# The last group's second product in seven parts, with its first product interleaved, in a fused retention and squared-ReLU kernel

## The chip, the cores and the metric

The kernel runs on one core of one Trainium2 chip. The metric is the device time of one execution, in microseconds (us); several executions are taken of each kernel, the kernel before and the changed one on the same chip, and the medians are quoted. The span of a profile is about 2 us shorter than the time of the same execution.

Engine names in the profile: PE is TensorE (matrix products), PEld its weight loads, DVE is VectorE, ACT is ScalarE, POOL is GpSimd, SP is SyncE. A "q" behind an engine's name means its instruction queue, which also issues stores.

## The reference, cut to what matters

```python
attn_out = retention(q, k, v)                  # (8, 8, 576, 64)
x = attn_out.transpose(0, 2, 1, 3).reshape(4608, 512)
h = x @ w_in                                   # (4608, 2048)   "first product"
r = np.maximum(h, 0.0)
g = r * r
out = g @ w_out                                # (4608, 512)    "second product"
```

The 4608 rows are cut into 36 units of 128 rows. Two units make a group, so there are 18 groups. A unit is either 128 rows that lie together ("full") or two blocks of 64 rows from two batches ("tail"). The last group holds a full unit, 34, and a tail unit, 35.

## The kernel before

The kernel writes no fixed order. It registers tasks with an engine, a sort key, a duration and dependences; a small list scheduler in Python then fixes the order of instructions for each engine. The sort key decides which of several ready tasks goes first. From group 2 on, the second product of a group is done in seven smaller products of half by half by half (Strassen's scheme in Winograd's form) instead of eight, with sums of blocks on DVE. The last group is the exception: it has the plain second product.

```python
def add_ff(g):                       # first product, ReLU, square, second product
    base = us[0] * L
    ...
    on_act = n == 2 and g >= STRASSEN and fb in SQ_ACT        # 7 of 8 squares on ACT
    ...
    if STRASSEN <= g < len(groups) - 1:
        add_strassen(g, us, base2, sq)
        return
    for s, u in enumerate(us):       # plain second product: groups 0, 1 and the last
        cuts = [(0, DM)] if u != groups[-1][-1] else [(0, HM), (HM, DM)]
        ...                          # 16 matmuls of 512 columns, or 2 x 16 of 256
        nc.scalar.copy(out=tile_of["o", u][:, lo:hi], in_=tile_of["po", u, lo])
        ...                          # store, issued by ACT in the last group
```

PSUM is the memory into which TensorE writes its products; a bank is one piece of it. In the seven-part scheme three PSUM banks serve all parts. The parts run in the order 1, 7, 6, 2, 5, 3, 4, so that part 6 is the third in time, and parts 3 and 4 are the sixth and the seventh. Bank a takes parts 1, 6, 5 and 3 in turn, and the sum so far is copied out by ACT between them:

```python
p5 = product(5, 16, "a", summed(0), wT[0], ...)
c4 = on_act_copy("u4", "a", 21, [p5])
d22 = on_dve_add(uB, 1, "c", "u4", 22, [p7, c4], ("o",))
p3 = product(3, 20, "a", summed(3), wB[1, 1], ..., [c4])       # waits for the copy
c12 = add("ACT", base + 25, 0.37, f12, deps=[p3, d11])
p4 = product(4, 24, "c", raw(1, 1), wT[3], high, ..., [d22])   # waits for the addition
```

## Time and profile before

| | kernel before |
|---|---|
| time, median of the first 3 runs | 298.69 us (298.68 to 298.79) |
| span of the profiled run | 296.6 us |
| TensorE busy | 286.1 us (96%) |
| last matmul ends | 293.46 us |
| from there to the end of the span | 3.14 us |

The table reads like this: TensorE works to 293.46 us almost without a break, and then 3.14 us pass in which the last result is copied out of PSUM, stored, and the program ends. The views that show it are in the prediction. One more, the sums over a stretch of time, gives the load of the other engines while the last two groups are worked on (columns: stretch, its length, then busy time and number of instructions of PE, PEld, DVE, ACT and POOL, the granted clock, the DMA share and GB/s):

```profile
268.60:286.50 17.90, 17.90 (x165) 16.00 (x164) 5.10 (x12) 14.65 (x28) 0.00 (x0) 1.00 0.16 60
```

ACT is busy for 14.65 of 17.90 us and DVE for 5.10.

### The profile page before, as it was taken

Reading aid. Unit: us, or ns where it says so; the run is one execution under the profiler, and the core shown is the slowest. Engines: PE = TensorE matmul, PEld = TensorE weight load, DVE = VectorE, ACT = ScalarE, POOL = GpSimd, SP = SyncE. Lnnn points to the kernel's source line nnn. Section 1 sums busy time; section 2 is a strip of 40 time slices with the busy share of each in tenths; the row PEclk is TensorE's granted clock in tenths of the full one; section 3 lists DMA queues with packets and bytes.
Section 4 is the critical chain, followed back from the end, with each engine's and each line's share of the span. In section 5 each row is a group of like instructions: output and inputs, shape, how many; then the busy total and the mean of one; then the engine's idle time right before and its main releaser. Section 6 shows DMA issues by size and latency. Waiting matters only on the chain.

```text
span 296.6 us, 10048 instructions
## 1 busy us (share of the span) xinstructions
PE 286.1 (96%) x4320; PEld 233.5 (79%) x4320; DVE 196.2 (66%) x413; ACT 187.5 (63%) x354; POOL 93.9 (32%) x129
## 2 busy tenths in 40 slices
PE   8979999999989999999999999999999999999995
PEld 3558755688878888888788888788888888888874
DVE  4777469967495959593959596766786766462410
ACT  5257753474867676648576667756666666658861
POOL 4454384544232506062414142435141520000000
PEclk9999999999999999999999999999999999999999
DMA  7999998899999989999969698999898980101012
GB/s 205 326 373 385 361 270 220 207 202 180 200 148 216 195 195 169 212 196 199 180 163 160 157 190 206 206 201 205 142 215 140 219 133 32 73 3 71 2 71 73
DMA packets 139261, 54.14 MB, mean 183 GB/s; under 512 B 118096, under 2 KB 130640, under 8 KB 139216
## 3 DMA queue, kind: packets, MB, share of 16 engines
q1 hardware_dynamic: 138768, 52.97, 86.2%
q8 instruction: 34, 0.56, 0.8%
q10 hardware_dynamic: 448, 0.52, 0.6%
q14 instruction: 11, 0.09, 0.1%
HBM read 36.70 MB, written 9.44 MB: 156 GB/s over the span
## 4 chain that ended last, share of the span: by engine, by line
PE 64%; DVE 11%; ACT 10%; DMA 9%; issue 2%; POOL 2%; POOLq 0%
PE po L912 26%; PE ph L819 25%; DVE gS L890 5%; ACT rl L827 5%; ACT gT L837 4%; PE psO L337 4%; PE po L860 4%; DMA pair<-in_v_dram 3%; DMA wo<-in_moe_w_out_dram 3%; DMA pair<-in_k_dram 3%; PE warm L241 2%; DVE gT L839 2%; PE psc L337 1%; PE psS L337 1%; PE psT L412 1%
## 5 line engine op out<-in xcount | busy, mean ns | idle before, releaser
L819 PE MATMUL ph<-xT,w_in 128*128 128x256 f16 x1152 | 139.3, 273 | 0.0
L819 PEld LDWEIGHTS <-w_in 128*128 128x128 f16 x1152 | 111.2, 98 | 14.8 <-POOL w_in L316 0.3
L827 ACT ACTIVATE rl<-ph 128x512 f16<-128x512 f32 x144 | 84.1, 588 | 51.4 <-PE ph L819 48.9
L837 ACT ACTIVATE gT<-rl 128x512 f16<-128x512 f16 x112 | 70.6, 630 | 3.4
L890 DVE TENSOR_TENSOR gS<-gT 128x512 f16<-128x512 f16 x60 | 31.8, 531 | 40.3 <-ACT gT L837 39.7
L912 PEld LDWEIGHTS <-gS 128*128 128x128 f16 x480 | 45.6, 98 | 9.8 <-DVE gS L890 4.5
L912 PE MATMUL po<-wT,gS 128*128 128x256 f16 x360 | 49.2, 273 | 2.0 <-DVE gS L890 1.9
L361 POOL TENSOR_TENSOR v<-v,vdec_full 128x512 f16<-128x512 f32 x24 | 26.2, 1092 | 58.4 <-DMA v<-in_v_dram 51.0
L912 PEld LDWEIGHTS <-gT 128*128 128x128 f16 x360 | 34.7, 98 | 4.2
L912 PE MATMUL po<-w_out,gT 128*128 128x256 f16 x240 | 31.1, 273 | 0.0
L349 POOL CAST kq<-k 128x512 f16<-128x512 f32 x28 | 19.0, 677 | 36.9 <-DMA k<-in_k_dram 35.6
L839 DVE TENSOR_TENSOR gT<-rl 128x512 f16<-128x512 f16 x32 | 18.1, 568 | 13.8 <-ACT rl L827 13.4
L349 POOL CAST kq<-q 128x512 f16<-128x512 f32 x28 | 18.1, 647 | 23.3 <-DMA q<-in_q_dram 23.2
L860 PE MATMUL po<-w_out,gT 128*128 128x512 f16 (+1 forms) x112 | 22.6, 349 | 0.1
L925 ACT COPY u<-po 128x256 f32<-128x256 f32 x30 | 11.0, 367 | 15.5 <-PE po L912 15.4
L935 DVE TENSOR_TENSOR o<-po,u 128x256 f32<-128x256 f32 x30 | 12.6, 419 | 11.8 <-PE po L912 8.1
L698 DVE TENSOR_TENSOR xT<-psO,gam_full 128x512 f16<-128x512 f32 x28 | 18.4, 684 | 2.7 <-PE psO L337 2.5
L637 DVE TENSOR_TENSOR rT<-psc,mask 128x512 f16<-128x512 f32 x28 | 18.5, 681 | 1.4 <-PE psc L337 1.4
L890 DVE TENSOR_TENSOR gS<-gS,gT 128x512 f16<-128x512 f16 x30 | 16.3, 544 | 1.0
L860 PEld LDWEIGHTS <-gT 128*128 128x128 f16 x112 | 10.6, 98 | 7.9 <-issue 0.2
L912 PE MATMUL po<-wT,gT 128*128 128x256 f16 x120 | 15.8, 273 | 0.0
L890 DVE TENSOR_TENSOR gS<-gT,gS 128x512 f16<-128x512 f16 x30 | 15.1, 505 | 1.0
(78 smaller groups left out, 264.2 us busy)
## 6 DMA issues: line engine op xcount, KB each, us to landing
out_dram<-o SPq DMA_DIRECT2D x31, 256.0 KB, 3.1
k<-in_k_dram SPq DMA_DIRECT2D x24, 256.0 KB, 4.9
q<-in_q_dram SPq DMA_DIRECT2D x24, 256.0 KB, 4.9
v<-in_v_dram SPq DMA_DIRECT2D x24, 256.0 KB, 4.6
wi<-in_moe_w_in_dram SPq DMA_DIRECT2D x4, 1024.0 KB, 9.9
wo<-in_moe_w_out_dram SPq DMA_DIRECT2D x4, 1024.0 KB, 9.5
pair<-in_k_dram SPq DMA_DIRECT2D x4, 512.0 KB, 5.7
pair<-in_q_dram SPq DMA_DIRECT2D x4, 512.0 KB, 5.4
```

Source lines behind the costliest of these rows:

```text
L337: nc.tensor.matmul(out_, lhsT=lhsT, rhs=rhs, start=start, stop=True, skip_group_check=True, tile_position=(64 * row, 64 * col))
L349: op(out=out_.rearrange("p (n b a d) -> p n b a d", n=2, b=2, a=2), in_=in_.rearrange("p (n a b) d -> p n b a d", n=2, a=2))
L361: nc.gpsimd.tensor_tensor(out=t, in0=tile_of["v32", u], in1=vdec[kind].rearrange("p (h o) -> p h o", o=1).to_broadcast([P, H, D]), op=ALU. ...
L637: nc.vector.tensor_tensor(out=r, in0=tile_of["psc", g][:, :, cols(s)].rearrange("p a (n i) -> p a n i", i=64), in1=mask.rearrange("p (o r ...
L698: nc.vector.tensor_tensor(out=tile_of["x", g][:, :, s * P:(s + 1) * P].rearrange("p n (c i) -> p c n i", c=2), in0=tile_of["psO", g][:, :, ...
L819: nc.tensor.matmul(tile_of["ph", g, fb][:, j, :], lhsT=w_in16[:, m, fi * P:(fi + 1) * P], rhs=tile_of["x", g][:, m, :], start=(m == 0), st ...
L827: nc.scalar.activation(out=t, in_=tile_of["ph", g, fb], func=ACTF.Relu)
L837: nc.scalar.activation(out=t, in_=rl, func=ACTF.Square)
L839: nc.vector.tensor_tensor(out=t, in0=rl, in1=rl, op=ALU.mult)
L860: nc.tensor.matmul(tile_of["po", u, lo], lhsT=tile_of["g", g][:, fi, s * P:(s + 1) * P], rhs=w_out16[:, fi, lo:hi], start=(fi == 0), stop= ...
L890: nc.vector.tensor_tensor(out=Sx(k, h), in0=in0(h), in1=in1(h), op=op)
L912: nc.tensor.matmul(tile_of["pb", g, bank], lhsT=left(i), rhs=right[:, i, :], start=(start and i == 0), stop=(i == HF - 1), skip_group_chec ...
```

## The change

The intent is to save an eighth of the last group's second product, the only one since group 2 that was still plain. That product stands at the very end, so two things are added to keep TensorE from waiting there. The last group's first product is interleaved with the second product of the group in front, so that its squares are ready sooner; and parts 3 and 4 get banks of their own, so that they need not wait for a copy or an addition. The squares of the last two groups move mostly from ACT to DVE, and the outputs are stored in quarters, as each becomes ready, half from ACT and half from SP.

```diff
+    SPREAD = 0.9
+    SQ_LATE = (1, 4, 6)
...
-        base = us[0] * L
+        base = min(us) * L
+        def place(x):
+            return base + x if g < last_g else base - NF * n - 1 + SPREAD * x
...
-            on_act = n == 2 and g >= STRASSEN and fb in SQ_ACT
+            on_act = g >= STRASSEN and fb in (SQ_ACT if g < last_g - 1 else SQ_LATE)
...
-        if STRASSEN <= g < len(groups) - 1:
+        if STRASSEN <= g:
             add_strassen(g, us, base2, sq)
             return
... (in add_strassen)
+        if g == last_g:
+            d7 = add("DVE", base + 18, 0.42, f7, deps=[p7, c2], acq=("p1",))     # p1 <- bank c + u2
+            d22 = on_dve_add(uB, 1, "c", "u4", 22, [c4, d7])
+            p3 = product(3, 20, "d", summed(3), wB[1, 1], lambda h: [s4[h]], True, True, [])
+            p4 = product(4, 24, "e", raw(1, 1), wT[3], high, True, True, [])
+            c12 = on_dve_add(uA, 1, "d", "u4", 25, [p3, d22])
+            d21 = on_dve_add(uB, 0, "e", "p1", 29, [p4, d22])
+        else:
             ...                                       # as before
+                for d in ds:
+                    lo = 0 if d in (d11, d21) else HM
+                    eng = ("ACT", ...) if d in (c12, d22) else ("SP", ...)
+                    ...                               # one store for each quarter
```

Here uA is the tail unit 35 and uB the full unit 34. Each store of a quarter of the tail unit is two instructions, one for each block of 64 rows.

More of the change, by code (lines that the diff above doesn't have):

```diff
@@ L784, with store @@
     wT_done = t1 + t2 + t3 + t4
-    def store(u, o, lo=0, hi=DM):
+    def store(u, o, lo=0, hi=DM, eng=nc.sync):
         kind, b, c = units[u]
-        eng = nc.scalar if group_of[u] == len(groups) - 1 else nc.sync
         if kind == "full":
@@ L820, in f @@
                                          rhs=tile_of["x", g][:, m, :], start=(m == 0), stop=(m == NP - 1))
-                f1.append(add("PE", base + (nf * fb + j) * n, 0.01 + 0.2133 * n, f,
+                f1.append(add("PE", place((nf * fb + j) * n), 0.01 + 0.2133 * n, f,
                               deps=[T["x", u] for u in us] + wcast_of(nf * fb + j) + f1[-1:],
@@ L839, in fg @@
                     nc.vector.tensor_tensor(out=t, in0=rl, in1=rl, op=ALU.mult)
-            r = add("ACT", base + 4 * fb + 4, 0.6, fr, deps=[f1[-1]], acq=("rl",))
+            r = add("ACT", place(4 * fb + 4), 0.6, fr, deps=[f1[-1]], acq=("rl",))
             sched.free("ff", [r])
-            sq.append(add("ACT" if on_act else "DVE", base + 4 * fb + 6, 0.63 if on_act else 0.45, fg, deps=[r] + sq[:1],
+            sq.append(add("ACT" if on_act else "DVE", place(4 * fb + 6), 0.63 if on_act else 0.45, fg, deps=[r] + sq[:1],
                           acq=() if fb else ("g",)))
@@ L852, in add_ff @@
             f2 = T["ff2"][-1:] if s == 0 else f2[-1:]
-            cuts = [(0, DM)] if u != groups[-1][-1] else [(0, HM), (HM, DM)]
-            for ci, (lo, hi) in enumerate(cuts):
-                for fi in range(NF):
-                    def f(fi=fi, s=s, u=u, lo=lo, hi=hi):
-                        if fi == 0:
-                            tile_of["po", u, lo] = ps_ff.tile([P, hi - lo], FP32, name="po", tag="ff")
-                        nc.tensor.matmul(tile_of["po", u, lo], lhsT=tile_of["g", g][:, fi, s * P:(s + 1) * P],
-                                         rhs=w_out16[:, fi, lo:hi], start=(fi == 0), stop=(fi == NF - 1))
-                    f2.append(add("PE", base2 + NF * s + fi / len(cuts) + 8 * ci, 0.0025 + 0.2135 / len(cuts), f,
-                                  deps=[sq[fi // nf]] + wcast[4 + fi // 4] + f2[-1:],
-                                  acq=("ff",) if fi == 0 else ()))
-                def fo(u=u, lo=lo, hi=hi):
-                    if lo == 0:
-                        tile_of["o", u] = o_pool.tile([P, DM], FP32, name="o", tag="o")
-                    nc.scalar.copy(out=tile_of["o", u][:, lo:hi], in_=tile_of["po", u, lo])
-                oc = add("ACT", end + 1, 0.12 + 0.47 / len(cuts), fo, deps=[f2[-1]], acq=() if lo else ("o",))
-                sched.free("ff", [oc])
-                st = add(*(("ACT", end + 1.1, 0.05) if g == len(groups) - 1 else ("SP", -0.5, 0.7)),
-                         lambda u=u, lo=lo, hi=hi: store(u, tile_of["o", u], lo, hi), deps=[oc], after=2.5)
@@ new lines, in add_ff, with f @@
+            for fi in range(NF):
+                def f(fi=fi, s=s, u=u):
+                    if fi == 0:
+                        tile_of["po", u] = ps_ff.tile([P, DM], FP32, name="po", tag="ff")
+                    nc.tensor.matmul(tile_of["po", u], lhsT=tile_of["g", g][:, fi, s * P:(s + 1) * P],
+                                     rhs=w_out16[:, fi, :], start=(fi == 0), stop=(fi == NF - 1))
+                f2.append(add("PE", base2 + NF * s + fi, 0.216, f, deps=[sq[fi // nf]] + wcast[4 + fi // 4] + f2[-1:],
+                              acq=("ff",) if fi == 0 else ()))
@@ L874, in add_ff, with fo @@
+            def fo(u=u):
+                tile_of["o", u] = o_pool.tile([P, DM], FP32, name="o", tag="o")
+                nc.scalar.copy(out=tile_of["o", u], in_=tile_of["po", u])
+            oc = add("ACT", end + 1, 0.59, fo, deps=[f2[-1]], acq=("o",))
+            sched.free("ff", [oc])
+            st = add("SP", -0.5, 0.7, lambda u=u: store(u, tile_of["o", u]), deps=[oc], after=2.5)
             sched.free("o", [st])
@@ L949, in add_strassen, with f7, f12 @@
         c4 = on_act_copy("u4", "a", 21, [p5])
-        d22 = on_dve_add(uB, 1, "c", "u4", 22, [p7, c4], ("o",))
-        sched.free("u4", [d22])
-        p3 = product(3, 20, "a", summed(3), wB[1, 1], lambda h: [s4[h]], False, True, [c4])
-        def f12():
-            nc.scalar.copy(out=o_tile(uA)[:, HM:], in_=bank("a"))
-        c12 = add("ACT", base + 25, 0.37, f12, deps=[p3, d11])
-        sched.free("ff", [c12])
-        p4 = product(4, 24, "c", raw(1, 1), wT[3], high, False, True, [d22])
-        d21 = on_dve_add(uB, 0, "c", "u2", 29, [p4, d22])
-        sched.free("ff", [d21])
-        sched.free("u2", [d21])
+        if g == last_g:
+            def f7():
+                t = tile_of["p1", g] = u_pool.tile([P, HM], FP32, name="p1", tag="p1")
+                nc.vector.tensor_tensor(out=t, in0=bank("c"), in1=tile_of["u2", g], op=ALU.add)
+            d7 = add("DVE", base + 18, 0.42, f7, deps=[p7, c2], acq=("p1",))
+            sched.free("u2", [d7])
+            d22 = on_dve_add(uB, 1, "c", "u4", 22, [c4, d7])
+            sched.free("ff", [d22])
+            sched.free("ff", [c4])
+            p3 = product(3, 20, "d", summed(3), wB[1, 1], lambda h: [s4[h]], True, True, [])
+            p4 = product(4, 24, "e", raw(1, 1), wT[3], high, True, True, [])
+            c12 = on_dve_add(uA, 1, "d", "u4", 25, [p3, d22])
+            d21 = on_dve_add(uB, 0, "e", "p1", 29, [p4, d22])
+            d22["acq"] = ("o",)
+        else:
+            d22 = on_dve_add(uB, 1, "c", "u4", 22, [p7, c4], ("o",))
+            sched.free("u4", [d22])
+            p3 = product(3, 20, "a", summed(3), wB[1, 1], lambda h: [s4[h]], False, True, [c4])
+            def f12():
+                nc.scalar.copy(out=o_tile(uA)[:, HM:], in_=bank("a"))
+            c12 = add("ACT", base + 25, 0.37, f12, deps=[p3, d11])
+            sched.free("ff", [c12])
+            p4 = product(4, 24, "c", raw(1, 1), wT[3], high, False, True, [d22])
+            d21 = on_dve_add(uB, 0, "c", "u2", 29, [p4, d22])
+            sched.free("ff", [d21])
+            sched.free("u2", [d21])
         sched.free("wst", [p3])
@@ L965, in add_strassen @@
         for u, ds in ((uA, [d11, c12]), (uB, [d22, d21])):
-            st = add("SP", -0.5, 0.7, lambda u=u: store(u, o_tile(u)), deps=ds, after=2.5)
-            sched.free("o", [st])
+            if g < last_g:
+                st = [add("SP", -0.5, 0.7, lambda u=u: store(u, o_tile(u)), deps=ds, after=2.5)]
+            else:
+                st = []
+                for d in ds:
+                    lo = 0 if d in (d11, d21) else HM
+                    eng = ("ACT", base + 25.1, 0.05) if d in (c12, d22) else ("SP", -0.5, 0.05)
+                    st.append(add(*eng, lambda u=u, lo=lo, eng=eng: store(u, o_tile(u), lo, lo + HM,
+                                                                          nc.scalar if eng[0] == "ACT" else nc.sync),
+                                  deps=[d], after=2.5))
+            sched.free("o", st)
     for g in range(len(groups)):
```

## The prediction

> **What bounds the kernel now.** I read the page first: the share of each engine and the slices over the span.
>
> ```profile
> PE 286.1 (96%) x4320; PEld 233.5 (79%) x4320; DVE 196.2 (66%) x413; ACT 187.5 (63%) x354; POOL 93.9 (32%) x129
> ...
> PE   8979999999989999999999999999999999999995
> ```
>
> TensorE is busy for 96% of a span of 296.6 us and falls only in the last slice. A busy TensorE is not proof of a bound, so I went on to the chain of work that ended last, from 255 us to the end. Its columns are the start, the length and the work.
>
> ```profile
> 268.60 4.80 PE ph L819 x44
> 273.40 1.75 PE po L912 x16
> 275.15 1.31 PE ph L819 x12
> 276.46 0.44 PE po L912 x4
> 276.89 0.87 PE ph L819 x8
> ...
> 281.26 1.75 PE po L912 x16
> 283.01 3.49 PE ph L819 x32
> 286.50 6.96 PE po L860 x48
> 293.46 0.02 issue
> 293.48 0.37 ACT o L869
> ```
>
> Each piece begins where the one before it ended, and all of them are TensorE until 293.46 us. There is no wait to be removed here: the end moves only if TensorE is given less to do, or if what follows its last matmul changes. The first product (ph) has a steady pace: 4.80 / 44 = 0.1091 us for one matmul of 256 columns. The last row is the last group's second product: 16 matmuls of 512 columns for one unit, then 2 x 16 of 256 for the other. At 0.1091 us the 32 narrow ones take 3.49 us, so the 16 wide ones take 6.96 - 3.49 = 3.47 us, 0.217 us each: a column costs the same in both widths.
>
> Third, the timeline of the last microseconds (start, length, engine, work):
>
> ```profile
> 286.34 7.11 PE L860 MATMUL po<-w_out,gT 128*128 128x512 f16 x48
> 286.84 0.63 ACT L837 ACTIVATE gT<-rl 128x512 f16<-128x512 f16 x1
> 287.37 0.58 ACT L827 ACTIVATE rl<-ph 128x512 f16<-128x512 f32 x1
> 287.99 0.43 DVE L839 TENSOR_TENSOR gT<-rl 128x512 f16<-128x512 f16 x1 [4.52 <-ACT rl L827]
> ...
> 293.48 0.37 ACT L869 COPY o<-po 128x256 f32<-128x256 f32 x1 [1.19 <-PE po L860]
> 293.88 0.34 ACTq L792 DMA_DIRECT2D out_dram<-o  x1
> ```
>
> From the last matmul's end to the end of the span there are 296.6 - 293.46 = 3.14 us: the copy out of PSUM ends at 293.85, the store is issued at 293.88, and 2.72 us follow. The view of DMA issues, from 293.8 us on, says how much of that is the store itself:
>
> ```profile
> out_dram<-o ACTq DMA_DIRECT2D x1, 128.0 KB, 1.7
> ```
>
> The store lands 1.7 us after its issue, which leaves 1.0 us in which the program ends. The rows also show that the first product of the last group hands over its last square at 288.4 us, 2 us into the second product. The plain second product takes the blocks in order, so this lateness costs nothing today. The new product wants the late blocks sooner.
>
> **What the Trainium skill says.** "TensorE: Matmul & The Clock Gate", section "Back-to-back issue gap", gives N / 2.4 + 2.5 ns as the isolated gap of a warm matmul, which is 109.2 ns for 256 columns and 215.8 ns for 512. The trace agrees: 109.1 and 217 ns. The same section gives about 131 ns as the sustained spacing at 512 columns; this trace does not show that, and I use the trace. "Perfetto Trace Analysis", section "Matmuls", says that independent matmul groups should rotate through different PSUM banks, so that the emptying of one overlaps the matmuls of the next; banks of their own for the last two parts are that rule. "DMA: Bandwidth & Descriptors", section "Issuing engines are not separate DMA queues", says that stores issued from two engines share the same 16 DMA engines and that only sequencer time is saved. No row of the trace before tests that, since its last stores all come from one queue.
>
> **The change part by part.**
>
> *Second product in seven parts.* The old one streams 16 x 512 + 32 x 256 = 16,384 columns. The new one has 7 products of 8 matmuls of 256 columns, 56 x 256 = 14,336 columns. The difference is that of 8 narrow matmuls: 8 x 0.1091 = 0.87 us off TensorE, in the one place where every microsecond is on the path. The new length is 56 x 0.1091 = 6.11 us.
>
> *Additions.* DVE gets 8 sums of 128x512 (0.42 to 0.43 us each in rows of this kind) and 5 additions of 128x256 (0.42 us), and more squares: 10 of the 16 squares of the last two groups go to DVE instead of 2. That is 8 x 0.43 + 5 x 0.42 + 8 x 0.43 = 9.0 us more on DVE. From 268.6 to 286.5 us DVE was busy 5.1 us of 17.9, so there is room. ACT loses 8 squares (5.0 us) and the output copies, and gains three 0.37 us copies. None of it is on the path unless TensorE waits for it.
>
> *Interleaving.* The order of instructions in the built program confirms it: the last group's 64 first-product matmuls are spread in fours and eights among the 56 of the group in front, and only 2 matmuls of that group follow the last of them. Nothing is removed by this. It makes the squares ready earlier relative to the second product, which the sums need.
>
> *Does TensorE wait?* I laid the last rows out by hand, with zero at the end of the last first-product matmul. TensorE then has 2 matmuls of the group in front, 8 of the first part, 8 of the second, and 4 of the third before it needs the last sum: 22 x 0.1091 = 2.40 us. On the other side: ReLU 0.04 to 0.64; DVE first does an output addition that waits for the 2 matmuls (0.25 to 0.67); square to 1.12; the sum with the late blocks to 1.58; the sum built on it to 2.04. That is 0.36 us early. The remaining waits are looser: the bank of the last part was freed by an addition that follows the fourth part, over 1 us earlier, and the parts that share a bank with a copy have a whole other part (0.87 us) between them, against 0.37 us of copying. Earlier in the interleaved stretch the closest wait is a bank that a ReLU must empty, some 0.4 us ahead. So I expect no TensorE wait, and the 0.87 us arrive.
>
> *After the last matmul.* Before: 0.02 + 0.37 (ACT copy) + 0.03 + 2.72 = 3.14 us. After: 0.03 + 0.42 (DVE addition) + 0.03 + 2.72 = 3.20 us, now through the SP queue. Just ahead of it ACT issues the tail unit's right half as two stores. Two such issues took 1.20 us before, so the second begins about 0.2 us after the last matmul and ends about 0.8 us after it; it lands at nearly the same moment as the last store. Three stores of 128 KB then meet in about 1.4 us; at the 330 to 346 GB/s that the last store reached alone, each occupies 0.4 us. I add 0.05 us for that. The loss is 0.11 us.
>
> Sum: -0.87 + 0.06 + 0.05 = -0.76 us, and 298.69 - 0.76 = 297.9 us.
>
> **The rivals.**
>
> First, **a wait takes the place of the removed work**: the sums or a bank come late and TensorE stands before the third part. For it: the slack is only 0.36 us, less than one ACT instruction (0.6 us), and both ACT and DVE run in order with other groups' work between. Against it: ACT had all of its first-product work, with 7 squares in a group, and still kept up to within 2 us; it is now relieved. One ACT instruction in the way would cost 0.6 - 0.36 = 0.24 us, giving 298.2 us; two would cost 0.84 us and leave 298.8 us.
>
> Second, **the tail grows**: the pair on the ACT queue, or the SP queue's own wait, lands after the last addition's store. For it: the rows of stores in two pieces show 0.55 to 0.60 us of issue for each piece against 0.35 us for a whole one. Against it: they start earlier. If the pair's second piece landed 2.3 us after its issue, the shortest that the trace shows for such pieces, it would do so at 0.2 + 2.3 = 2.5 us, against 0.48 + 1.7 = 2.2 us for the last store. That would add 0.3 us: 298.2 us.
>
> Third, **the interleaving itself pays or costs**: TensorE changes bank and weights source every 2 to 8 matmuls. Pieces of 4 in the chain before took 0.44 us, the steady pace, so I give it nothing. Nor can it pay by filling gaps, since the chain has none there. If each of some 25 changes cost 10 ns, the time would be 298.1 us.
>
> **Range and chances.** The main term is a count times a steady pace, so it can hardly be off by more than 0.05 us. The rivals all take back, by 0.2 to 0.8 us; a few tenths can also be gained if the end of the program is shorter after the SP queue. I take 297.5 to 298.4 us. A change of 2% would need 6 us, several times all that is being moved, so within 2% is nearly certain.
>
> **What would show it right or wrong.** Right: the chain shows 56 matmuls in about 6.1 us at the end with no wait on ACT or DVE between them; TensorE's last matmul ends near 292.6 us; DVE's last addition is 0.42 us and some 2.7 us follow its store. Wrong, first rival: a gap before the third part, with DVE sums named as its releaser. Wrong, second: over 3.4 us from the last matmul to the end. Wrong, third: the interleaved stretch runs slower than 0.109 us a matmul. The prediction as a whole fails if the time is not 0.3 to 1.2 us lower.

## The result

The changed kernel took 299.25 us in the median of six runs (298.73 to 299.64), the kernel before 298.69 us (298.44 to 298.79) in six runs on the same chip. The ratio of the changed kernel's time to that of the one before is 1.0019, with a 95% interval of 1.0007 to 1.0032. A ratio is the mean time of one kernel's fast runs over that of the other's of the same rounds, so it is not quite the ratio of the medians. The time lies above the predicted range (297.5 to 298.4 us), and the direction is the opposite of the predicted one.

The profiled run is the fastest of the six (298.73 us). First the page's busy times:

```profile
PE 284.7 (96%) x4328; PEld 234.0 (79%) x4328; DVE 205.3 (69%) x434; ACT 182.9 (62%) x346; POOL 93.2 (31%) x129
```

DVE has 9.1 us more than before (9.0 were predicted) and ACT 4.6 us less (squares of 5.0 us were to leave it). The sums over the same stretch as above, now with DVE at 9.14 us, show that the moved work found room:

```profile
268.62:286.30 17.68, 17.68 (x164) 15.85 (x163) 9.14 (x23) 12.00 (x22) 0.00 (x0) 1.00 0.08 31
```

The chain of work that ended last (start, length, work), in the stretch that the change reorders:

```profile
281.50 0.22 PE po L910 x2
281.72 0.44 PE ph L823 x4
282.15 0.22 PE po L910 x2
...
284.34 1.53 PE po L910 x14
285.87 0.44 PE ph L823 x4
286.30 6.35 PE po L910 x58
292.65 0.02 issue
292.67 0.42 DVE o L933
```

The interleaving stands there, mostly in twos and fours, at the same 0.109 us a matmul, and no other engine comes between. The last 58 matmuls (2 of the group in front and 56 of the seven parts) take 6.35 us. The last matmul ends at 292.65 us. This is the predicted place (292.6), and 0.81 us earlier than before.

So the gain arrived on TensorE and is lost behind it. From the last matmul to the end of the span there are now 296.4 - 292.65 = 3.75 us instead of 3.14. The timeline of these last microseconds:

```profile
291.79 0.38 ACTq L792 DMA_DIRECT2D out_dram<-o  x1
292.26 1.17 ACTq L796 DMA_DIRECT2D out_dram<-o  x2
292.67 0.42 DVE L933 TENSOR_TENSOR o<-po,p 128x256 f32<-128x256 f32 x1 [0.45 <-PE po L910]
293.12 0.34 SPq L792 DMA_DIRECT2D out_dram<-o  x1
```

The last store is issued at 293.12, and 3.28 us follow it (2.72 before). The second line is the tail unit's right half, two stores by ACT, whose issues last until 293.43: the "late pair" from here on. The view of DMA issues from 288 us on (size of one, us from issue to landing):

```profile
out_dram<-o SPq DMA_DIRECT2D x2, 64.0 KB, 2.0
out_dram<-o ACTq DMA_DIRECT2D x1, 128.0 KB, 1.8
out_dram<-o ACTq DMA_DIRECT2D x2, 64.0 KB, 2.1
out_dram<-o SPq DMA_DIRECT2D x1, 128.0 KB, 2.2
```

The last store takes 2.2 us to land; the last store of the kernel before took 1.7.

A gain of 0.8 us and a loss of 0.6 us leave 0.2 us less, but the median is 0.56 us more. The profiled run, the fastest of the six, can't show why. There are thus two questions: what makes the end longer, and where the rest comes from.

### The profile page after: what moved, and what is told of

Its sections match the earlier page's. It is cut to its first block, busy times and chain, and to the rows that moved or that the text cites. A ratio compares the mean times of both kernels' runs of the same rounds, so it can differ in the third digit from the quotient of the medians.

```text
span 296.4 us, 10095 instructions
## 1 busy us (share of the span) xinstructions
PE 284.7 (96%) x4328; PEld 234.0 (79%) x4328; DVE 205.3 (69%) x434; ACT 182.9 (62%) x346; POOL 93.2 (31%) x129
## 4 chain that ended last, share of the span: by engine, by line
PE 62%; DVE 12%; DMA 11%; ACT 8%; issue 3%; POOL 2%; SPq 0%; POOLq 0%; DVEq 0%
PE po L910 27%; PE ph L823 27%; DVE gS L888 5%; ACT rl L831 4%; PE psO L339 4%; ACT gT L841 4%; DMA wo<-in_moe_w_out_dram 3%; DMA pair<-in_v_dram 3%; DMA pair<-in_k_dram 3%; DMA pair<-in_q_dram 2%; PE psc L339 1%; DVE gT L843 1%; PE po L861 1%; PE psS L339 1%; DVE o L933 1%
## 5 line engine op out<-in xcount | busy, mean ns | idle before, releaser
L841 ACT ACTIVATE gT<-rl 128x512 f16<-128x512 f16 x104 | 65.5, 630 | 3.2
L910 PEld LDWEIGHTS <-gS 128*128 128x128 f16 x512 | 48.9, 98 | 9.6 <-DVE gS L888 3.9
L910 PE MATMUL po<-wT,gS 128*128 128x256 f16 x384 | 53.0, 273 | 1.7 <-DVE gS L888 1.3
L910 PEld LDWEIGHTS <-gT 128*128 128x128 f16 x384 | 37.2, 98 | 4.9 <-issue 0.3
L910 PE MATMUL po<-w_out,gT 128*128 128x256 f16 x256 | 33.5, 273 | 0.0
L843 DVE TENSOR_TENSOR gT<-rl 128x512 f16<-128x512 f16 x40 | 21.0, 527 | 15.2 <-ACT rl L831 14.7
L888 DVE TENSOR_TENSOR gS<-gT,gS 128x512 f16<-128x512 f16 x32 | 18.6, 585 | 1.0
L888 DVE TENSOR_TENSOR gS<-gS,gT 128x512 f16<-128x512 f16 x32 | 17.8, 556 | 1.1
L910 PE MATMUL po<-w_out,gS 128*128 128x256 f16 x128 | 16.6, 273 | 0.0
L861 PE MATMUL po<-w_out,gT 128*128 128x512 f16 x64 | 15.5, 379 | 0.2 <-POOL w_out L318 0.2
```

Source lines behind the costliest of these rows:

```text
L841: nc.scalar.activation(out=t, in_=rl, func=ACTF.Square)
L843: nc.vector.tensor_tensor(out=t, in0=rl, in1=rl, op=ALU.mult)
L861: nc.tensor.matmul(tile_of["po", u], lhsT=tile_of["g", g][:, fi, s * P:(s + 1) * P], rhs=w_out16[:, fi, :], start=(fi == 0), stop=(fi == N ...
L888: nc.vector.tensor_tensor(out=Sx(k, h), in0=in0(h), in1=in1(h), op=op)
L910: nc.tensor.matmul(tile_of["pb", g, bank], lhsT=left(i), rhs=right[:, i, :], start=(start and i == 0), stop=(i == HF - 1), skip_group_chec ...
```

## The experiments

Two numbers serve for all of them. The first is the **matmul stretch**, from the start of the last retention output products, which stand ahead of everything the change touches, to the end of the last matmul. The second is the **tail**, from there to the end of the span. The start is read in the timeline as the first row of this kind, here in the kernel before and in the changed one:

```profile
261.82 0.21 PE L337 MATMUL psO<-kqT,Rm 64*64 64x64 f16 x1
```

```profile
261.84 0.21 PE L339 MATMUL psO<-kqT,Rm 64*64 64x64 f16 x1
```

The stretch is 293.46 - 261.82 = 31.64 us before and 292.65 - 261.84 = 30.81 us after. All that both numbers leave out is the same program in both kernels: the order of instructions in the built programs is equal up to that point on every engine.

| run | edit | start, us | stretch, us | tail, us | sum, us |
|---|---|---|---|---|---|
| before | | 261.82 | 31.64 | 3.14 | 34.78 |
| b1_before | none, again | 262.90 | 31.63 | 3.07 | 34.70 |
| b3_inter | interleaving alone | 262.58 | 31.64 | 3.08 | 34.72 |
| after | the change | 261.84 | 30.81 | 3.75 | 34.56 |
| a1_again | none, again | 260.35 | 30.80 | 3.85 | 34.65 |
| c4_after | none, again | 261.07 | 30.80 | 3.73 | 34.53 |
| a2_queues | issuing engines exchanged | 262.96 | 30.81 | 3.73 | 34.54 |
| a3_nopair | late pair left out | 262.16 | 30.81 | 3.13 | 33.94 |
| b4_full | late pair doubled in bytes | 262.08 | 30.80 | 4.02 | 34.82 |
| c2_tiny | late pair, few bytes | 262.14 | 30.80 | 3.56 | 34.36 |
| d2_tinysplit | few bytes, two engines | 261.64 | 30.81 | 3.35 | 34.16 |
| b2_split, c3_split | late pair from two engines | 262.14, 262.41 | 30.80, 30.81 | 3.36, 3.28 | 34.16, 34.09 |
| d1_one | late pair as one store | 262.20 | 30.80 | 5.60 | 36.40 |
| a4_nointer | without the interleaving | 261.70 | 31.17 | 3.83 | 35.00 |
| c1_banks | without banks of their own | 262.44 | 31.42 | 3.74 | 35.16 |

The views print a span to 0.1 us, so a tail or a sum of the table can be off by 0.05 us. Read unrounded from the kept traces, the tail is 3.12 to 3.13 us in the kernel before, b1_before and b3_inter, 3.78 to 3.82 in the changed kernel, a1_again and c4_after, 3.16 in a3_nopair, 3.71 in a2_queues, 3.54 in c2_tiny, 3.32 in d2_tinysplit, and 3.33 and 3.34 in b2_split and c3_split. Equal programs thus repeat the stretch within 0.02 us and the tail within 0.04 us. The start moves by 2.6 us between executions, although nothing in front of it differs.

### a1_again, b1_before and c4_after: both kernels once more

The edit is none: the changed kernel twice more, and the kernel before as a run of its own. The question is whether 0.56 us slower is a property of the change.

> The changed kernel unaltered, for a second trace: the first trace fell in its fastest execution (298.73 us, where the median is 299.25). Theory A (the loss is in the stores after the last matmul, several of which are under way at once): the last matmul ends near 292.7 us again and 4.2 to 4.8 us follow it, against 3.75 in the first trace. Theory C (the loss is somewhere earlier in the program, from the loads or instruction fetch, and varies): the last matmul ends 0.4 to 0.9 us later than 292.65 and about 3.7 us follow. Time 299.0 to 299.4 under both.

> The kernel before, as a run of its own, for a second trace of it and for the spread of its times beside its own copies. From the start of the last output products that both kernels share (261.82 us in the first trace) to the last matmul: 31.64 us again, within 0.05; from the last matmul to the end 3.14 us, within 0.1. If that start itself moves by up to 1 us or more between traces, as it did in the four traces of the changed kernel and its variants (260.35 to 262.96), then the spread of the whole time belongs to the part that the change doesn't touch, and the two kernels can be told apart by the two stretches alone. Ratio to its own copies: 1.000, within the interval.

> The changed kernel unaltered, a third set of times. If the first comparison (0.56 us slower in the median) was due to the spread of the untouched part, the ratio lies within 0.997 and 1.003 with both signs possible, and the stretches are 30.81 and 3.75 to 3.85 us again. If the change really slows the untouched part, the ratio comes out at 1.001 or more a second time and the start of the shared products, as the difference of the span and the two stretches, lies 0.5 us or more above that of the kernel before.

Measured, as medians: a1_again 297.94 us against 298.42, ratio 0.9995 (0.9959 to 1.0031); c4_after 298.33 us against 298.90, ratio 0.9990 (0.9965 to 1.0014); b1_before 299.38 us against 298.98 for copies of itself, ratio 1.0009 (0.9981 to 1.0037). The stretches came out as expected. In a1_again neither theory's picture held: the tail was 3.85 us, a little below the 4.2 asked of theory A, and the start was 1.5 us earlier rather than later.

In these rounds the kernel before ranged from 296.98 to 299.70 us on one chip, 298.01 to 300.11 on another. With the two stretches known, each run's start can be worked out as its span less the sum in the table. For a1_again to a4_nointer (24 runs) the mean start is 261.62 us, and for the kernel before on that chip (11 runs, sum taken as 34.74, the mean of its two traces) it is 261.63, the difference being -0.02 with a 95% interval of 0.53 either way. For b2_split and b4_full (12 runs) against the kernel before, b1_before and b3_inter (23 runs) it is -0.02, 0.39 either way. For the four runs of the third call (20) against the kernel before (11) it is -0.08, 0.44 either way. For d1_one (6 against 11) it is -0.14, 0.5 either way. Most of these runs are variants, but all have the same program up to the start. So no slowing of the part that the change doesn't touch is seen; the first three together leave room for some 0.26 us either way. In the first comparison the six runs of the changed kernel give starts from 261.8 to 262.9 us (span less 34.6), mean 262.5, while the kernel before, by its times, stayed within 0.35 us. No later session repeats that difference; why that one showed it, and why the kernel before was so steady there, is open.

What moves the start is partly seen in the waits between 60 and 270 us. This is the line for TensorE's weight loads that wait for block sums, in the changed kernel and in a2_queues, whose start is 1.1 us later (total wait, times, longest):

```profile
PEld L910 <- DVE gS L888: 3.9, 8, 0.7
```

```profile
PEld L910 <- DVE gS L888: 4.3, 8, 0.9
```

In a1_again, with the earliest start, the same waits come to 2.6 us. The kernel before has 4.5 us at nearly the start of the changed one (261.82), so these waits are not the whole of it. But groups in the middle of the program wait for sums more or less long from one execution to the next. What decides it in an execution was not settled.

### a3_nopair: the late pair left out

```diff
                 for d in ds:
+                    if d is c12:
+                        continue
```

The result is wrong: 128 rows lack their right half.

> Wrong on purpose: the tail unit's right half (two pieces, 128 KB) is never stored; everything else stands. Theory A: the last store has only one neighbour left, lands 1.7 to 1.9 us after its issue, and the time falls to 298.0 to 298.5 us. Theory B (the queue of the last store): unchanged, 299.0 to 299.4 us. Theory C (loss earlier than the tail): unchanged as well.

The tail fell to 3.13 us, that of the kernel before. The DMA issues of this run:

```profile
out_dram<-o SPq DMA_DIRECT2D x1, 128.0 KB, 1.7
```

The last store lands in 1.7 us again, although SP issues it and DVE makes its data. So the whole loss of the tail comes from the late pair, and neither from the SP queue nor from DVE in place of ACT. The time, 297.82 us against 298.42 (ratio 0.9983, 0.9950 to 1.0016), agrees but is too spread to show it alone.

### a2_queues: the issuing engines exchanged

```diff
-  eng = ("ACT", base + 25.1, 0.05) if d in (c12, d22) else ("SP", -0.5, 0.05)
+  eng = ("ACT", base + 25.1, 0.05) if d in (d21, d22) else ("SP", -0.5, 0.05)
```

> The two issuing engines of the last stores exchanged: the tail unit's right half (two pieces) from SP, the last store from ACT, as in the kernel before. Theory A (stores share the DMA engines, whoever issues them): no change, 299.0 to 299.4 us, landing of the last store still over 2.1 us. Theory B (a store from the SP queue takes longer to land, or stands behind the queue's earlier ones): the last store lands 1.7 us after its issue as before, and the time falls to 298.3 to 298.6 us.

The tail was 3.73 us. Which engine issues the last store makes no difference; theory B falls. The time was 298.05 us against 298.42 (ratio 0.9990, 0.9956 to 1.0024): the range expected under A, 299.0 to 299.4, was missed because the expectation took the first session's level for the kernel's own. The times of a1_again and a4_nointer missed their ranges for the same reason, and a3_nopair (297.82) lay just under its own.

### b2_split and c3_split: the late pair from two engines

```diff
                 r0 = (b + i) * S + 512
-                eng.dma_start(out=out[r0:r0 + 64, lo:hi], in_=o[i * 64:(i + 1) * 64, lo:hi])
+                (nc.sync if i and eng is nc.scalar else eng).dma_start(
+                    out=out[r0:r0 + 64, lo:hi], in_=o[i * 64:(i + 1) * 64, lo:hi])
```

> The changed kernel, with the tail unit's right half stored from two engines, one piece each, so that the second piece is issued 0.6 us earlier. Theory A (the last store shares the DMA engines with the second piece, because that piece is issued late): the last store lands about 1.7 to 1.8 us after its issue instead of 2.2, and the stretch from the last matmul to the end falls from 3.75-3.85 to 3.2-3.35 us. Theory A2 (the number of stores or bytes of the last 3 us is what counts, whenever they are issued): 3.7 to 3.9 us again. To the last matmul 30.81 us under both.

> The changed kernel with the pair's two pieces issued from two engines, a second time, on a chip with the unchanged change beside it. Last matmul to end 3.36 us (0.1 either way), stretch before it 30.80 us; the sum is 0.45 us below that of the changed kernel and 0.6 us below that of the kernel before. In the whole time the difference to the kernel before should come out between 0 and -1.2 us, since the untouched part spreads by about 0.7 us from run to run.

The two pieces are now issued side by side, so the second starts 0.6 us earlier. The bytes and the number of stores are unchanged. The tail fell to 3.36 and 3.28 us. From the timeline of b2_split:

```profile
292.56 0.54 ACTq L796 DMA_DIRECT2D out_dram<-o  x1
292.97 0.42 DVE L933 TENSOR_TENSOR o<-po,p 128x256 f32<-128x256 f32 x1 [0.45 <-PE po L910]
293.42 0.34 SPq L792 DMA_DIRECT2D out_dram<-o  x1
```

ACT's piece has been issued by 293.10, ahead of the last store, which then lands in 1.8 us. Theory A2, by which the number of bytes and stores in the last 3 us counts whenever they are issued, falls.

In the whole time b2_split took 298.33 us against 298.98 (ratio 0.9979, 0.9956 to 1.0002) and c3_split 297.76 us against 298.90 (ratio 0.9969, 0.9947 to 0.9991). This version is correct and is below both kernels, by about 0.6 us against the kernel before (34.74 - 34.12 in the sums) and 0.45 us against the change (34.58 - 34.12, each the mean of its traces).

### b4_full: the late pair doubled

```diff
                 for d in ds:
+                    if d is d11:
+                        continue
...                                    # c12's store takes lo = 0, hi = DM and waits for d11 too
```

The tail unit is stored once, in full rows, when its right half is ready.

> The changed kernel, with the tail unit stored once, in full rows, when its right half is ready: the pair that collides with the last store is doubled from 2 x 64 KB to 2 x 128 KB, the same total is stored. Theory A (sharing with the late pair): the last store lands 2.4 to 2.8 us after its issue and last matmul to end grows to 3.9-4.4 us. If the number of packets counts and not the bytes (full rows are 2 KB instead of 1 KB, the number of packets of the pair stays): unchanged at 3.7-3.9 us.

The tail grew to 4.02 us and the last store landed late:

```profile
out_dram<-o SPq DMA_DIRECT2D x1, 128.0 KB, 2.6
```

The pair keeps its moment and the number of its rows; only its bytes double. So bytes count when they are late. The time was 299.06 us against 298.98 (ratio 1.0009, 0.9985 to 1.0033).

### c2_tiny and d2_tinysplit: is it the bytes or the issues?

```diff
                 r0 = (b + i) * S + 512
+                if eng is nc.scalar:
+                    hi = lo + 16
```

Both are wrong: of each row of the late pair only 16 columns are stored, 4 KB a piece. In d2_tinysplit the pieces come from two engines as in b2_split.

> Wrong on purpose: the late pair keeps its two pieces of 64 rows, its engine and its moment, but each row carries 16 columns instead of 256 (4 KB a piece instead of 64). Theory A (the bytes of the late pair share the DMA engines with the last store): the last store lands 1.7 to 1.8 us after its issue, last matmul to end 3.1 to 3.3 us. Theory E (two engines make descriptors at the same time, and the last store's have to wait): the landing stays at 2.2 us and the end at 3.7 to 3.9 us.

> Wrong on purpose: the pair's pieces carry 16 columns, and each is issued from an engine of its own, so that both issues are over before the last store's begins. If the 0.4 us that were left with the small pieces come from issues that overlap that of the last store: last matmul to end 3.1 to 3.2 us, as without the pair, and the last store lands 1.7 us after its issue. If any store in flight delays the last one: 3.4 to 3.6 us.

The last store in the view of DMA issues, first in c2_tiny, then in d2_tinysplit:

```profile
out_dram<-o SPq DMA_DIRECT2D x1, 128.0 KB, 2.0
```

```profile
out_dram<-o SPq DMA_DIRECT2D x1, 128.0 KB, 1.7
```

With few bytes, but the same two issues one after the other, the tail was 3.56 us and the last store landed in 2.0 us. That is neither of the two expected pictures: of the 0.6 to 0.7 us that the pair costs, 0.2 us go away with its bytes, and some 0.4 us stay. When the issues are over sooner as well (d2_tinysplit), the last store lands in 1.7 us as expected, but the tail is 3.35 us, between the two expected pictures. In all, the runs share the loss between the bytes that are under way late (c2_tiny, b4_full) and the late second issue, which overlaps that of the last store (d2_tinysplit against c2_tiny; whether the overlap counts, or the 64 small rows that follow it late, is not separated).

A rest of about 0.2 us stays with any pair in flight, and the kept traces show where most of it lies: behind the last landing. Unrounded, the span ends 0.96 us after the last landing in the kernel before, a3_nopair and b4_full, but 1.08 to 1.09 us after it in the changed kernel, c2_tiny, d2_tinysplit, b2_split and c3_split. From the landing on, SP goes through its closing waits for the semaphores (counters by which engines and stores tell each other that they are done) of the stores, three in the first kind of run (0.18 to 0.19 us) and five in the second (0.32 us), although by then all of them have been met. That is 0.13 us. No run changed the number of these waits alone. c2_tiny's time was 298.42 us against 298.90 (ratio 0.9997, 0.9970 to 1.0024).

### d1_one: one store for both blocks

```diff
+        elif eng is nc.scalar:
+            eng.dma_start(out=out.rearrange("(n s) m -> n s m", s=S)[b:b + 2, 512:576, lo:hi], in_=o[:, lo:hi])
```

> The changed kernel, with the tail unit's right half stored by one instruction over both of its row blocks instead of two. The bytes and the engine stay; the issue should take about 0.4 to 0.6 us instead of 1.17 and end before the last store is issued. If the lateness of the second piece and the overlap of the issues make the loss: last matmul to end 3.2 to 3.4 us, as with the pieces on two engines. If the bytes of the last 3 us do it: 3.6 to 3.8 us. Last output products up to the last matmul 30.80 us.

This was to be the best version and is the worst. From its timeline and its DMA issues:

```profile
292.62 1.13 ACTq L794 DMA_DIRECT2D out_dram<-o  x1
```

```profile
out_dram<-o SPq DMA_DIRECT2D x1, 128.0 KB, 3.7
```

One instruction over a pattern of 2 x 64 rows takes 1.13 us to issue, as long as the two instructions did, and the last store behind it lands only after 3.7 us. In the last 1.6 us before its landing no more than 34 to 60 GB/s moved, by the GB/s row of the DMA view. The tail was 5.60 us and the time 300.04 us against 298.51 (ratio 1.0048, 1.0019 to 1.0078). The expectation of a shorter issue had no measurement behind it. The kept trace shows more. This one store itself lands last of all, 4.64 us after the last matmul, where the last store lands at 4.22. After the last matmul ACT's queue moved 256 rows and 18 packets of 4 bytes, 16 for the store ahead and 2 for the pair, where the changed kernel has 48 for its three stores there, 16 for each. Of the last store's 16 reports of landing, 14 had come by 3.27 us and the other two came at 4.22. I infer that two of the 16 DMA engines carried the whole pair and held up the last store's share on them; no run tests this.

### b3_inter: the interleaving alone

The kernel before with `place`, `SPREAD` and `SQ_LATE` of the change, and the plain second product.

> Only the interleaving, with the second product of the last group as before (512 and 256 columns, copies by ACT, stores from ACT). Prediction's view: TensorE has the same matmuls as before and no gaps to fill, so start of the shared products to last matmul 31.64 us, within 0.1, last matmul to end 3.14 us, within 0.1: no gain and no loss. If changing weights and banks every 2 to 8 matmuls costs something, the first number rises by 0.1 to 0.3 us.

Stretch 31.64 us and tail 3.08 us: nothing gained, nothing lost, as expected. Changing the bank and the weights every 2 to 8 matmuls costs nothing that shows. The time was 298.78 us against 298.98 (ratio 0.9997, 0.9970 to 1.0025).

### a4_nointer: the seven parts without the interleaving

```diff
-            return base + x if g < last_g else base - NF * n - 1 + SPREAD * x
+            return base + x
```

> The seven parts without the interleaving: the last group's first product keeps its old place in the order. The hand-laid sums say that the last sum is ready about 2.0 us after the last first-product matmul and is wanted 20 matmuls (2.2 us) after it, so TensorE should hardly wait: last matmul within 0.2 us of that of the full change, time within 0.2 us of it (299.0 to 299.4 us). If the interleaving is what makes the seven parts possible, a wait of 0.3 us or more for the sums shows before the third part, and the time is higher by as much.

The stretch was 31.17 us, 0.36 us longer. I had expected at most 0.2. The end of its timeline shows the wait for the last sum, before the second half of the third part:

```profile
287.35 0.42 DVE L843 TENSOR_TENSOR gT<-rl 128x512 f16<-128x512 f16 x1
287.80 0.42 DVE L888 TENSOR_TENSOR gS<-gT 128x512 f16<-128x512 f16 x1
288.26 0.43 DVE L888 TENSOR_TENSOR gS<-gS,gT 128x512 f16<-128x512 f16 x1
288.72 0.43 DVE L888 TENSOR_TENSOR gS<-gT,gS 128x512 f16<-128x512 f16 x1
288.75 0.61 PE L910 MATMUL po<-wT,gS 128*128 128x256 f16 x4 [0.18 <-DVE gS L888]
```

The last ReLU had run from 286.71 us because ACT was a square behind, not at once after the last first-product matmul; that is what my 2.0 us had left out. Of the 0.36 us the wait itself is 0.18; the rest is TensorE starting anew, which c1_banks below shows too. So the interleaving is worth 0.36 us to the seven parts and nothing by itself. The time was 298.51 us against 298.42 (ratio 0.9999, 0.9967 to 1.0032).

### c1_banks: without banks of their own

```diff
-        if g == last_g:
+        if False:
```

> The changed kernel without banks of its own for the sixth and seventh part: the last group uses the same three banks as the groups ahead of it, so that the sixth part has to wait for the ACT copy of the fifth. Worked out from the rows of the changed kernel: 0.03 + 0.37 + 0.03 us of wait at that place, start of the shared products to last matmul 30.81 + 0.43 = 31.24 us (0.1 either way); last matmul to end 3.7 to 3.9 us as in the changed kernel. If the copy is hidden (the part order gives it time), 30.8 us.

The stretch was 31.42 us, 0.61 us longer than in the change; 0.43 had been expected. The sixth part waits for the copy:

```profile
291.52 0.37 ACT L923 COPY u<-po 128x256 f32<-128x256 f32 x1 [1.38 <-PE po L910]
291.92 0.42 DVE L933 TENSOR_TENSOR o<-po,u 128x256 f32<-128x256 f32 x1 [0.80 <-ACT u L923]
291.94 1.03 PE L910 MATMUL po<-w_out,gS 128*128 128x256 f16 x8 [0.46 <-ACT u L923]
```

The wait itself is 0.44 us in the chain. The other 0.17 us are TensorE starting anew: the 16 matmuls after the wait take 1.92 us in the chain, where 16 take 1.75 us without one. This fits the page's figures: one matmul's record lasts 273 ns, the spacing in a stream is 109 ns, and the first after a wait has none before it to overlap with. So own banks are worth 0.61 us, and the tail is not changed by them (3.74 us). The time was 298.39 us against 298.90 (ratio 0.9984, 0.9958 to 1.0010).

## Why the prediction was wrong

**Bound and gain: right.** TensorE set the pace, nothing came between, and the seven parts took 0.83 us off the stretch (31.64 to 30.81), where 0.87 were predicted.

**TensorE does not wait: right, and for the reason given.** The last sum was ready 2.01 us after the last first-product matmul (2.04 worked out). The first matmul that reads it starts at 2.24 us, not at 2.40, so the slack was nearer to 0.2 us than to 0.36. It was small, as the prediction said: taking the interleaving or the banks away costs 0.36 and 0.61 us. The first rival did not come about.

**The interleaving itself costs and pays nothing: right** (b3_inter). The third rival did not come about. (Its sum has a slip: 297.93 + 0.25 is 298.2, not 298.1.)

**The step that failed is "After the last matmul".** It saw the late pair, placed its second issue rightly (predicted to end 0.8 us after the last matmul, measured 293.43 - 292.65 = 0.78), and then priced the meeting of the stores at 0.05 us by the rate at which they move. "The loss is 0.11 us" measured 0.6 to 0.7 us (3.73 to 3.85 us of tail over 3.07 to 3.14). Two terms were mis-sized. The landing of the last store grew from 1.74 to 2.24 us, 0.5 us in place of 0.05. And what follows the landing, taken over unchanged in the 2.72 us, grew by 0.13 us, with SP's two more waits. The addition on DVE and the SP queue were priced rightly: without the pair the tail is 3.13 us, where 3.20 was worked out. The second rival, that the tail grows, is what happened. It was on paper with 0.3 us; the true size is twice that. It also named the wrong store: not the pair's landing ended the program later, but the landing of the last store, stretched by the pair.

**A second thing was wrong: the width of the range.** It allowed for the rivals and not for the spread of the time itself; the three runs at hand lay within 0.11 us. Equal programs were later seen from 296.98 to 299.70 us on one chip, nearly all of it in the 262 us that the change doesn't touch. With -0.83 + 0.65 = -0.18 us of true difference, a median of six runs can fall on either side; in the first comparison it fell 0.56 us high, in two later ones 0.48 and 0.57 us low, so the sign of a single comparison is luck. That the change as such is slower is not shown, and the traces speak against it.

## What to carry to other kernels

When matrix work is taken from the very end of a program, what follows the last matmul must be worked out with the same care. Here two stores issued close ahead of the last one cost more than their bytes: their late issue counted too, and moving the second 0.6 us forward, by issuing the two from two engines, recovered two thirds of the loss. Compare small changes by stretches of the trace that repeat within hundredths of a microsecond, not by whole times that, as here, spread by two microseconds and more. A rearrangement that gains nothing alone (the interleaving; the banks were not tried alone) may still be what lets another change keep its gain, and only undoing it in place shows how much.

## What the Trainium skill lacked or had wrong

- "TensorE: Matmul & The Clock Gate", section "Back-to-back issue gap": about 131 ns as the sustained spacing of matmuls of 512 columns is not what this kernel shows; 16 of them took 3.47 us, 217 ns each, as the section's formula for the isolated gap has it. The formula also fits 256 columns (109 ns).
- "DMA: Bandwidth & Descriptors", section "Issuing engines are not separate DMA queues": that the engine of issue doesn't matter to the transfer agrees (tail 3.73 us with the engines exchanged, 3.75 without). That several engines save only issue time, usually small relative to the DMA, hides how much that can be at the end of a program: issuing two pieces from two engines shortened the tail by about 0.45 us here.
- "Perfetto Trace Analysis", section "Matmuls": that independent groups should rotate through PSUM banks agrees, and has a size here: 0.61 us for one place without it.
- No page was found that has the issue times by shape seen here: 0.34 to 0.38 us for a store of 128 rows of 256 columns, about 0.5 to 0.6 us for one of 64 rows, 1.13 us for one store over 2 x 64 rows.
- No page was found that has the cost of the closing waits for stores that have already landed: 0.32 us for five in place of 0.19 us for three, at the end of the program.
